# Two gated MLPs after attention: the operand sums of each layer in half steps

## The chip, the core and the metric

The kernel runs on one core of a Trainium2 chip. The engines that count here are TensorE (PE in the profile; PEld are its weight loads), VectorE (DVE), ScalarE (ACT) and the queue of SyncE that issues the DMAs (SP). Each works through its own instructions in the order written and is held up only where it waits for another. The metric is the device time of one execution in microseconds (us), lower is better.

## The reference

```python
def rmsnorm(x, g):
    return x / np.sqrt(np.mean(x * x, axis=-1, keepdims=True) + 1e-06) * g
# q, k, v: (4, 12, 448, 64)
scores = np.matmul(rmsnorm(q, g_q), rmsnorm(k, g_k).transpose(0, 1, 3, 2)) / np.sqrt(64)
attn = softmax(scores)                       # over the last axis
x = np.matmul(attn, v)                       # to (1792, 768): tokens x features
x = ((x @ w_a) * (x @ w_b)) @ w_out          # first MLP, d_ff = 1536
x = (sigmoid(x @ w_gate) * (x @ w_val)) @ w_out2   # second MLP, the same sizes
```

q, k and v are float32. The weights are float64, and the chip turns their words into float32 (the decode).

## The kernel before

**Products.** Attention runs first, then the two MLPs, each in two parts: a first part (up to the gated product) and a second part (with w_out). A matrix product is done by a seven-product scheme on 2 x 2 blocks. The first part's left operands are, with the four blocks A11, A12, A21, A22 of the transposed activations (384 features x 896 tokens each, that is KC = 3 chunks of 128 x 896): A11, A12 and A22 themselves, and S1 = A21 + A22, S2 = S1 - A11, S3 = A11 - A21, S4 = A12 - S2. To keep float32 accuracy, every operand is split in two float32r tiles, a high part (a cast on ScalarE) and a low part (operand minus high part, on VectorE): `xh`, `xl` for the left operands, `wh`, `wl` for the weights.

**Order of the products.** A list `events`, written by hand, gives the order of the products (m, p) of a first part: m is a pair of weight columns, p one of seven products. It begins (0,1), (1,1), (0,2), (2,1), (1,2), (3,1), (2,2), (3,2), (0,5), (0,6), (1,5), (0,7), (0,3), (1,6), ... Products p = 1 need A11, p = 2 A12, p = 5 S1, p = 6 S2, p = 7 S3, p = 3 S4, p = 4 A22. So the first eight work on blocks that are there, and S1 is first wanted by (0,5), S2 by (0,6). A product is six groups of three matmuls (high x high, low x high, high x low): the three chunks on 512 columns, then on 384.

**Banks.** Product (m,2) adds to the PSUM bank that (m,1) filled; between them ScalarE copies the bank into a tile `u` (line 1045, "the eviction of (m,1)"), with which line 967 later seeds the bank of (m,6). So (m,2) can't begin before the eviction of (m,1) is done. Line 1017 multiplies an odd m's result with the even one's (a gate), 1047, 1049, 1052 are other evictions.

**Weights.** `prepare` is called after each group of matmuls and writes the next step of the weights' decode (lines 693 on ScalarE, 694, 696, 700 on VectorE), of the differences of weight blocks (801, 805), and of the splits: the cast to `wh` (813, ScalarE) and `wl` (627, `rest`, VectorE).

**The operands.** `operands(l)` is a generator that writes S1 to S4 of MLP l (and, in the first MLP, a copy of A22), one chunk at a time, between the groups of matmuls: `first_part` counts the groups in `ticks` and advances the generator at every 4th, later at every 5th or 6th. Before, one advance (a step) writes: the low part of a chunk whose cast was written a step earlier, the cast of the chunk that was summed a step earlier, and this chunk's sum. `casts` and `rests` hold what is still owed. In the trace the sums are line 905, the casts line 896, the low parts line 627 (`xl`). `stage_in` loads the blocks from DRAM into the places of tiles that come to be free (`fl`, `fh` in the first MLP; `al`, `ah` are sums that the second one finds on the chip). Where the operands aren't ready when a product is written, the generator is run at once (`urgent`).

Of the kernel before, what the change touches and what calls it, by code (L numbers as in the profile page):

```python
# [14 lines left out]
ALU = mybir.AluOpType  # L15
# [8 lines left out]
def attention_then_two_gated_mlps(  # L24
# [69 lines left out]
    def place(n, half, c, dtype=F32R, name="x"):  # L94

        return places[n].tile([P, S2], dtype, tag=f"{half}{c}", name=f"{name}{half}")
# [515 lines left out]
    def take_u():  # L612
        tag = free_u.pop(0)
        return tag, ups[0].tile([P, S2], F32, tag=tag, name=tag)
# [11 lines left out]
    def rest(t, hi, lo, eng):  # L626
        eng.tensor_tensor(out=lo, in0=t, in1=f32(hi), op=ALU.subtract)  # L627
# [219 lines left out]
    def stage_in(l, n, c):  # L847

        at = where[l]
        t, half, spot, y = {"A21": (1, 0, "S4", "l"), "A11": (0, 0, "A22", "l"), "A22": (1, 1, "A22", "h"), "A12": (0, 1, "S4", "h")}[n]  # L850
        tile_ = place(at[spot], y, c, F32, "f")
        staged[l].setdefault(n, []).append(tile_)
        nc.sync.dma_start(out=tile_, in_=xd[l][t][KC * half + c])
# [24 lines left out]
    def operands(l):  # L878

        at = where[l]  # L880
        a, b, d = (staged[l][n] for n in ("A21", "A22", "A11"))
        casts, rests = [], []

        def flush(n=0):

            while rests and len(rests) + len(casts) > n:
                m, t, hi, lo, tag = rests.pop(0)
                rest(t, hi, lo, nc.vector)
                X.setdefault(m, []).append((hi, lo))
                if tag:  # L890
                    free_u.append(tag)
            while len(casts) > min(n, 1):
                m, c, t, tag = casts.pop(0)
                hi = place(at[m], "h", c)
                lo = place(at["A22" if (l, m) == (0, "S4") else "S4" if (l, m) == (0, "A22") else m], "l", c)
                nc.scalar.copy(out=hi, in_=t)
                rests.append((m, t, hi, lo, tag))
            if n == 0 and rests:
                flush()

        def to(m, c, t, tag=None):
            casts.append((m, c, t, tag))

        def tt(out, x, y, op):
            nc.vector.tensor_tensor(out=out, in0=x, in1=y, op=op)


        t = a if l == 0 else b
        for c in range(KC):
            flush(2)  # L910
            tt(t[c], a[c], b[c], ALU.add)
            to("S1", c, t[c])
            if l == 0:
                stage_in(0, "A12", c)
            yield
        for c in range(KC):
            flush(2)
            tt(t[c], t[c], d[c], ALU.subtract)
            to("S2", c, t[c])
            yield  # L920
        for c in range(KC):
            flush(2)
            if l == 0:
                tt(t[c], staged[l]["A12"][c], t[c], ALU.subtract)
                to("S4", c, t[c])
                yield
                continue
            while len(free_u) < (1 if urgent else 3):
                flush()
                yield  # L930
            tag, u = take_u()
            tt(u, d[c], a[c], ALU.subtract)
            tt(t[c], staged[l]["A12"][c], t[c], ALU.subtract)
            to("S4", c, t[c])
            yield
            flush(1)
            to("S3", c, u, tag)
            yield
        flush()
        if l == 0:  # L940
            for c in range(KC):
                while len(free_u) < 1:
                    flush()
                    yield
                flush(1)
                tag, u = take_u()
                nc.scalar.copy(out=u, in_=b[c])
                to("A22", c, u, tag)
                yield
            flush()  # L950

    ready, urgent = [False], []

    def first_part(l, then):
# [15 lines left out]
        for e, (m, p) in enumerate(events):  # L970
# [18 lines left out]
            for o, size in HALVES:  # L989
                for c in range(KC):  # L990
                    hi, lo = X[n_][c]
                    for z, (w, x) in enumerate(((wh, hi), (wh, lo), (wl, hi))):
                        nc.tensor.matmul(  # L993
                            ps[:, o:o + size], w[:, P * c:P * c + P], x[:, o:o + size],
                            start=(p in (1, 5) and c == 0 and z == 0), stop=(c == KC - 1 and z == 2),
                            skip_group_check=p not in (1, 5),
                        )
                    prepare(l, min(e + AHEAD, NE - 1), 1)
                    if more is None and ready[0]:
                        more = operands(l)  # L1000
                    if more is not None:
                        ticks += 1
                        if ticks % ((5 if ticks > 24 else 4) if l else 6 if ticks > 12 else 4) == 0:
                            next(more, None)
                    if e >= NE - 4:
                        then(e - NE)
                    yield
# [407 lines left out]
```

## Time and profile before

| | |
|---|---|
| runs shown | 1212.5, 1213.63, 1213.7 us; median 1213.63 us |
| the profiled execution | 1212.98 us; span from first to last instruction 1211.2 us |
| PE busy | 1195.3 us, 99% of the span |
| DVE busy | 918.6 us, 76% |
| ACT busy | 655.4 us, 54% |
| first MLP, first part | starts at 269.18 us |
| second MLP, first part | starts at 740.37 us |

The profiled execution's own time lies 1.78 us over its span, and 0.65 us under the median of the runs. The engines' busy times overlap. Matmuls are pipelined, so that each lasts longer in the records than the distance to the next one's start; a row's idle time in brackets is counted from the end of the one before.

### The profile page before, as it was taken

How to read it: one execution, taken by the hardware profiler on the slowest of the kernel's cores; microseconds unless marked ns; L12 is line 12 of the kernel's file. 1: busy time of each engine (PE TensorE's matmuls, PEld its weight loads, DVE VectorE, ACT ScalarE, POOL GpSimd, SP SyncE). 2: the span in 40 equal slices, each digit the busy share in tenths (PEclk: the TensorE clock that was granted, in tenths of full speed). 3: DMA queues.
4: the chain of work that ended last, by engine and by line, in shares of the span. 5: the costliest groups of instructions: out<-in, count | busy, mean ns of one | idle time of the engine just before them, and what ended most of it. 6: DMA issues, size and time to landing. Idle time of an engine off the chain costs nothing.

```text
span 1211.2 us, 18283 instructions
## 1 busy us (share of the span) xinstructions
PE 1195.3 (99%) x6468; PEld 1013.9 (84%) x6468; DVE 918.6 (76%) x1625; ACT 655.4 (54%) x1276; POOL 157.7 (13%) x241
## 2 busy tenths in 40 slices
PE   8999999999999999999999999999999999999997
PEld 6666666658788888888888888888888888999997
DVE  8888888977868687785768688976786877666672
ACT  7787788864634433444455566544545444445542
POOL 5665668600000000000000000000000000000000
PEclk9999999999999999999999999999999999999999
DMA  5444455348136465654955753234564654777683
GB/s 134 134 137 118 124 151 159 100 148 308 48 126 189 146 194 161 189 190 139 319 183 185 244 178 116 78 133 130 173 202 142 200 162 143 270 252 242 198 257 96
DMA packets 142764, 205.78 MB, mean 170 GB/s; under 512 B 23208, under 2 KB 116560, under 8 KB 142672
## 3 DMA queue, kind: packets, MB, share of 16 engines
q1 hardware_dynamic: 142064, 204.18, 53.9%
q8 instruction: 51, 0.84, 0.3%
q10 hardware_dynamic: 480, 0.43, 0.1%
q14 instruction: 41, 0.34, 0.1%
q0 software_dynamic: 128, 0.00, 0.0%
HBM read 150.21 MB, written 54.35 MB: 169 GB/s over the span
## 4 chain that ended last, share of the span: by engine, by line
PE 89%; DVE 4%; DMA 3%; ACT 2%; issue 1%; SPq 1%; ACTq 0%; DVEq 0%
PE mm L993 46%; PE mm L1276 13%; PE mm L1286 10%; PE pv L410 6%; PE s L350 5%; PE tr L381 4%; PE tr L303 1%; DVE xl L627 1%; PE tr L378 1%; DMA fh<-xd 1%; PE tr L386 1%; DMA xd<-xs 1%; DMA u<-gd 1%; DVE wl L627 0%; DMA raw<-in_moe_w_a_dram 0%
## 5 line engine op out<-in xcount | busy, mean ns | idle before, releaser
L993 PE MATMUL mm<-xl,wh 128*128 128x512 f32 (+1 forms) x1008 | 369.0, 366 | 2.6 <-DVE xl L627 2.6
L993 PE MATMUL mm<-xh,wl 128*128 128x512 f32 (+1 forms) x1008 | 370.3, 367 | 0.7 <-DVE wl L627 0.7
L993 PE MATMUL mm<-xh,wh 128*128 128x512 f32 (+1 forms) x1008 | 368.2, 365 | 0.7 <-ACT u L1045 0.5
L993 PEld LDWEIGHTS mm<-xl,wh 128*128 128x128 f32 x1008 | 189.6, 188 | 26.3 <-DVE xl L627 3.5
L993 PEld LDWEIGHTS mm<-xh,wh 128*128 128x128 f32 x1008 | 189.9, 188 | 25.0 <-issue 1.4
L993 PEld LDWEIGHTS mm<-xh,wl 128*128 128x128 f32 x1008 | 189.5, 188 | 22.1 <-DVE wl L627 1.1
L627 DVE TENSOR_TENSOR wl<-d,wh 128x384 fp32r<-128x384 f32 x250 | 136.3, 552 | 64.7 <-ACT wh L1153 40.9
L813 ACT CAST wh<-d 128x384 fp32r<-128x384 f32 x166 | 82.0, 514 | 102.0 <-DVE d L801 81.6
L693 ACT ACTIVATE d<-raw 128x384 f32<-128x384 f32 x138 | 75.7, 555 | 80.9 <-DMA raw<-in_moe_w_out_dram 40.5
L700 DVE SCALAR_TENSOR_TENSOR d<-d,raw 128x384 uint32<-128x384 uint32 x138 | 77.5, 562 | 54.7 <-ACT d L693 49.1
L368 ACT ACTIVATE P<-s,nm 128x448 f32<-128x448 f32 x168 | 105.2, 635 | 5.7 <-DVE nm L356 5.1
L1153 ACT CAST wh<-d 128x384 fp32r<-128x384 f32 x84 | 43.2, 514 | 119.6 <-issue 36.8
L356 DVE TENSOR_REDUCE nm<-s 128x1 f32<-128x448 f32 x168 | 97.3, 613 | 3.1 <-PE s L350 3.1
L1286 PE MATMUL mm<-wh,gh 128*128 128x384 f32 x294 | 98.8, 336 | 0.3 <-ACT mm L1257 0.2
L1286 PE MATMUL mm<-wl,gh 128*128 128x384 f32 x294 | 98.6, 335 | 0.0
L1286 PE MATMUL mm<-wh,gl 128*128 128x384 f32 x294 | 98.5, 335 | 0.0
L1276 PE MATMUL mm<-gl,wh 128*128 128x512 f32 x252 | 92.6, 368 | 0.0
L1276 PE MATMUL mm<-gh,wl 128*128 128x512 f32 x252 | 92.4, 366 | 0.0
L1276 PE MATMUL mm<-gh,wh 128*128 128x512 f32 x252 | 91.7, 364 | 0.0
L696 DVE SCALAR_TENSOR_TENSOR raw<-raw 128x384 uint32<-128x384 uint32 x140 | 78.1, 558 | 4.0
L397 ACT COPY pt<-tr 128x512 f32<-128x512 f32 x96 | 54.9, 572 | 44.7 <-PE tr L381 42.1
L1063 DVE TENSOR_TENSOR u<-mm,u 128x896 f32<-128x896 f32 x48 | 52.2, 1087 | 27.9 <-PE mm L993 27.9
(161 smaller groups left out, 1949.4 us busy)
## 6 DMA issues: line engine op xcount, KB each, us to landing
gd<-u SPq DMA_DIRECT2D x60, 448.0 KB
u<-gd SPq DMA_DIRECT2D x60, 448.0 KB
d<-wd SPq DMA_DIRECT2D x132, 192.0 KB
raw<-in_moe_w_out_dram SPq DMA_DIRECT2D x48, 384.0 KB
wd<-d SPq DMA_DIRECT2D x72, 192.0 KB
raw<-in_moe_w_a_dram SPq DMA_DIRECT2D x24, 384.0 KB
raw<-in_moe_w_b_dram SPq DMA_DIRECT2D x24, 384.0 KB
raw<-in_moe_w_val_dram SPq DMA_DIRECT2D x23, 384.0 KB
```

The lines of the kernel that those rows point to most:

```text
L350: nc.tensor.matmul(out_, w[e, o:o + P], x[e, m:m + S], start=(n == 0), stop=(n == 2))
L356: nc.vector.tensor_reduce(out=d["nm"][:, t:t + 1], in_=d["ps"][t], axis=AX.X, op=ALU.max, negate=True)
L368: nc.scalar.activation(out=e, in_=d["ps"].pop(t), func=AF.Exp, bias=d["nm"][:, t:t + 1], accum_out=d["sum"][:, t:t + 1])
L410: nc.tensor.matmul(d["pv"][64 * h:64 * h + 64], w, x, start=(j == 0), stop=(j == R), skip_group_check=True)
L627: eng.tensor_tensor(out=lo, in0=t, in1=f32(hi), op=ALU.subtract)
L693: nc.scalar.activation(out=f32(t), in_=f32(high), func=AF.Copy, scale=2.0 ** -112)
L696: nc.vector.scalar_tensor_tensor(out=low, in0=high, scalar=0x80000000, in1=low, op0=ALU.bitwise_and, op1=ALU.bitwise_or)
L700: nc.vector.scalar_tensor_tensor(out=t, in0=t, scalar=3, in1=low, op0=ALU.logical_shift_left, op1=ALU.bitwise_or)
L813: nc.scalar.copy(out=hi, in_=t)
L993: nc.tensor.matmul(ps[:, o:o + size], w[:, P * c:P * c + P], x[:, o:o + size], start=(p in (1, 5) and c == 0 and z == 0), stop=(c == KC - ...
L1276: nc.tensor.matmul(ps[:, o:o + size], w[:, P * un:P * un + P], g[:, o:o + size], start=(p in (1, 5) and f == 0 and z == 0), stop=(f == HF ...
L1286: nc.tensor.matmul(ps[:, o:o + HB], g[:, P * t:P * t + P], w, start=(p in (1, 5) and f == 0 and z == 0), stop=(f == HF - 1 and z == 2), sk ...
```

## The change

The generator's step is cut in two halves. In one half it writes the low part of the chunk before and the sum of this one, in the other the cast of this one. A chunk's low part then comes in the half step after its cast, and its cast in the half step after its sum: one chunk is in work at a time, where before three were. The half steps come at every 2nd group, later at every 3rd (first MLP) or at two groups of five (second MLP), so that a chunk gets as many groups as before. In the second MLP S3's difference is a half step alone, and its cast and low part come after S4's of the same chunk. The loads, the products, their order and the number of sums and casts stay as they are.

```diff
--- before.py
+++ after.py
@@ -879,75 +879,71 @@
 
         at = where[l]
         a, b, d = (staged[l][n] for n in ("A21", "A22", "A11"))
-        casts, rests = [], []
-
-        def flush(n=0):
-
-            while rests and len(rests) + len(casts) > n:
-                m, t, hi, lo, tag = rests.pop(0)
-                rest(t, hi, lo, nc.vector)
-                X.setdefault(m, []).append((hi, lo))
-                if tag:
-                    free_u.append(tag)
-            while len(casts) > min(n, 1):
-                m, c, t, tag = casts.pop(0)
-                hi = place(at[m], "h", c)
-                lo = place(at["A22" if (l, m) == (0, "S4") else "S4" if (l, m) == (0, "A22") else m], "l", c)
-                nc.scalar.copy(out=hi, in_=t)
-                rests.append((m, t, hi, lo, tag))
-            if n == 0 and rests:
-                flush()
-
-        def to(m, c, t, tag=None):
-            casts.append((m, c, t, tag))
-
-        def tt(out, x, y, op):
+        t = a if l == 0 else b
+        spare_u = lambda: len(free_u) >= (1 if l == 0 or urgent else 3)
+
+        def tt(out, x, y, op=ALU.subtract):
             nc.vector.tensor_tensor(out=out, in0=x, in1=y, op=op)
 
-
-        t = a if l == 0 else b
-        for c in range(KC):
-            flush(2)
+        def s1(c):
             tt(t[c], a[c], b[c], ALU.add)
-            to("S1", c, t[c])
             if l == 0:
                 stage_in(0, "A12", c)
+            return t[c], None
+
+        def s2(c):
+            tt(t[c], t[c], d[c])
+            return t[c], None
+
+        def s4(c):
+            tt(t[c], staged[l]["A12"][c], t[c])
+            return t[c], None
+
+        def s3(c):
+            thirds[c] = tag, u = take_u()
+            tt(u, d[c], a[c])
+            return None, None
+
+        def s3_end(c):
+            return thirds.pop(c)[::-1]
+
+        def a22(c):
+            tag, u = take_u()
+            nc.scalar.copy(out=u, in_=b[c])
+            return u, tag
+
+        jobs = [(n, f, c) for n, f in (("S1", s1), ("S2", s2)) for c in range(KC)]
+        if l == 0:
+            jobs += [(n, f, c) for n, f in (("S4", s4), ("A22", a22)) for c in range(KC)]
+        else:
+            thirds.clear()
+            jobs += [(n, f, c) for c in range(KC) for n, f in ((None, s3), ("S4", s4), ("S3", s3_end))]
+        low_at = {"S4": "A22", "A22": "S4"} if l == 0 else {}
+        last = None
+
+        def low():
+            n, u, hi, lo, tag = last
+            rest(u, hi, lo, nc.vector)
+            X.setdefault(n, []).append((hi, lo))
+            if tag:
+                free_u.append(tag)
+
+        for n, make, c in jobs:
+            if last:
+                low()
+                last = None
+            while make in (s3, a22) and not spare_u():
+                yield
+            u, tag = make(c)
+            if make is not s3_end:
+                yield
+            if u is None:
+                continue
+            hi, lo = place(at[n], "h", c), place(at[low_at.get(n, n)], "l", c)
+            nc.scalar.copy(out=hi, in_=u)
+            last = n, u, hi, lo, tag
             yield
-        for c in range(KC):
-            flush(2)
-            tt(t[c], t[c], d[c], ALU.subtract)
-            to("S2", c, t[c])
-            yield
-        for c in range(KC):
-            flush(2)
-            if l == 0:
-                tt(t[c], staged[l]["A12"][c], t[c], ALU.subtract)
-                to("S4", c, t[c])
-                yield
-                continue
-            while len(free_u) < (1 if urgent else 3):
-                flush()
-                yield
-            tag, u = take_u()
-            tt(u, d[c], a[c], ALU.subtract)
-            tt(t[c], staged[l]["A12"][c], t[c], ALU.subtract)
-            to("S4", c, t[c])
-            yield
-            flush(1)
-            to("S3", c, u, tag)
-            yield
-        flush()
-        if l == 0:
-            for c in range(KC):
-                while len(free_u) < 1:
-                    flush()
-                    yield
-                flush(1)
-                tag, u = take_u()
-                nc.scalar.copy(out=u, in_=b[c])
-                to("A22", c, u, tag)
-                yield
-            flush()
+        low()
 
     ready, urgent = [False], []
 
@@ -1000,7 +996,7 @@
                         more = operands(l)
                     if more is not None:
                         ticks += 1
-                        if ticks % ((5 if ticks > 24 else 4) if l else 6 if ticks > 12 else 4) == 0:
+                        if ticks % 5 in (0, 2) if l and ticks > 24 else ticks % (2 if l or ticks <= 12 else 3) == 0:
                             next(more, None)
                     if e >= NE - 4:
                         then(e - NE)
```

The order of the matmuls, of GpSimd's work and of the DMAs is the same in both programs. What moves stands on ScalarE and VectorE. In the rows below the number behind a tile's name tells tiles apart; numbers of lines behind `operands` are four lower after the change (1045 is 1041 there, 1017 is 1013).

ScalarE in the first MLP, around the evictions of (2,1) and (3,1); `fl_4511`, `fl_4515`, `fl_4517` are chunks 0, 1, 2 of S1 and then of S2, and `u3`, `u2` take the evictions. Before:

```order
L1052 ACTIVATE u0_4596<-mm_4421 128x896
L813 CAST wh_4602<-u4_4377 128x384
L896 CAST xh_4612<-fl_4511 128x896
L1045 COPY u3_4627<-mm_4598 128x896
L813 CAST wh_4632<-d8_4545 128x384
L896 CAST xh_4643<-fl_4515 128x896
L813 CAST wh_4666<-d0_1025 128x384
L896 CAST xh_4674<-fl_4517 128x896
L1045 COPY u2_4687<-mm_4658 128x896
```

and now:

```order
L943 CAST xh_4578<-fl_4511 128x896
L943 CAST xh_4597<-fl_4515 128x896
L1048 ACTIVATE u0_4603<-mm_4421 128x896
L813 CAST wh_4609<-u4_4377 128x384
L943 CAST xh_4623<-fl_4517 128x896
L1041 COPY u3_4637<-mm_4605 128x896
L813 CAST wh_4642<-d8_4545 128x384
L943 CAST xh_4652<-fl_4511 128x896
L813 CAST wh_4676<-d0_1025 128x384
L943 CAST xh_4683<-fl_4515 128x896
L1041 COPY u2_4697<-mm_4668 128x896
```

The eviction of (2,1) (to `u3`) came behind the cast of S1's chunk 0 and now comes behind that of S1's chunk 2; that of (3,1) (to `u2`) came behind the cast of S1's chunk 2 and now comes behind that of S2's chunk 1.

VectorE in the same stretch, from the sum of S1's chunk 2 on; `mm_4531` is the bank of (1,2), whose gate goes to `u0`, `d0_1025` is the difference of weights for (0,5), and `wl` from `u4_4377` is that of (2,2). Before:

```order
L905 TENSOR_TENSOR fl_4517<-fl_4517,fh_4519 128x896
L627 TENSOR_TENSOR wl_4603<-u4_4377,wh_4602 128x384
L627 TENSOR_TENSOR xl_4613<-fl_4511,xh_4612 128x896
L905 TENSOR_TENSOR fl_4511<-fl_4511,fl_4521 128x896
L1017 TENSOR_TENSOR u0_4596<-mm_4531,u0_4596 128x896
L801 TENSOR_TENSOR d0_1025<-d1_2377,d0_1025 128x384
```

and now:

```order
L886 TENSOR_TENSOR fl_4517<-fl_4517,fh_4519 128x896
L627 TENSOR_TENSOR xl_4624<-fl_4517,xh_4623 128x896
L886 TENSOR_TENSOR fl_4511<-fl_4511,fl_4521 128x896
L627 TENSOR_TENSOR wl_4610<-u4_4377,wh_4609 128x384
L627 TENSOR_TENSOR xl_4653<-fl_4511,xh_4652 128x896
L886 TENSOR_TENSOR fl_4515<-fl_4515,fl_4523 128x896
L1013 TENSOR_TENSOR u0_4603<-mm_4531,u0_4603 128x896
L801 TENSOR_TENSOR d0_1025<-d1_2377,d0_1025 128x384
```

Three low parts (S1's chunks 1 and 2, S2's chunk 0) and the sum of S2's chunk 1 now stand ahead of the gate and of the difference of weights behind it, which did not before; ahead of the `wl` of (2,2) it is the three low parts of S1 and the sum of S2's chunk 0.

ScalarE in the second MLP, around the eviction of (3,1) (to `u1`); `al_7806`, `al_7814`, `al_7822` are the chunks of S1, S2 and then S4, `u3`, `u5` hold S3's, `d0_8527` is the difference of weights for (0,5). Before:

```order
L896 CAST xh_8802<-al_7814 128x896
L693 ACTIVATE d3_8811<-raw_8648 128x384
L896 CAST xh_8831<-al_7822 128x896
L813 CAST wh_8844<-d0_8527 128x384
L693 ACTIVATE d5_8851<-raw_8778 128x384
L896 CAST xh_8865<-al_7806 128x896
L1045 COPY u1_8874<-mm_8836 128x896
```

and now:

```order
L943 CAST xh_8797<-al_7822 128x896
L1041 COPY u6_8800<-mm_8761 128x896
L813 CAST wh_8805<-d7_8695 128x384
L693 ACTIVATE d3_8815<-raw_8648 128x384
L943 CAST xh_8835<-al_7806 128x896
L813 CAST wh_8848<-d0_8527 128x384
L943 CAST xh_8853<-u3_8810 128x896
L693 ACTIVATE d5_8859<-raw_8786 128x384
L1041 COPY u1_8878<-mm_8840 128x896
```

The casts ahead of the eviction were those of S2's chunks 1 and 2 and S4's chunk 0, with the weights' casts and decodes between; they now are those of S2's chunk 2, S4's chunk 0 and S3's chunk 0.

## Rows read from the trace of the kernel before

**Rows 1.** Page: busy time by engine; chain that ended last, shares of the span.

```profile
PE 1195.3 (99%) x6468; PEld 1013.9 (84%) x6468; DVE 918.6 (76%) x1625; ACT 655.4 (54%) x1276; POOL 157.7 (13%) x241
...
PE 89%; DVE 4%; DMA 3%; ACT 2%; issue 1%; SPq 1%; ACTq 0%; DVEq 0%
```

**Rows 2.** TensorE in order of time, first MLP: start us, us, line, operation [idle before <-releaser].

```profile
295.60 0.39 PE L993 MATMUL mm<-xh,wh 128*128 128x512 f32 x1
...
299.27 0.48 PE L993 MATMUL mm<-xh,wh 128*128 128x512 f32 x1
...
306.68 0.39 PE L993 MATMUL mm<-xh,wh 128*128 128x512 f32 x1
...
309.24 0.50 PE L993 MATMUL mm<-xl,wh 128*128 128x512 f32 x1 [1.47 <-DVE xl L627]
...
311.36 0.68 PE L993 MATMUL mm<-xl,wh 128*128 128x512 f32 x1 [1.16 <-DVE xl L627]
...
315.06 0.39 PE L993 MATMUL mm<-xh,wh 128*128 128x512 f32 x1
```

**Rows 3.** Stretches of 5 us: busy time (xinstructions) by engine, granted clock, DMA share, GB/s.

```profile
305.00:310.00 5.00, 3.53 (x18) 2.68 (x16) 4.96 (x7) 3.08 (x5) 0.00 (x0) 1.00 0.38 132
310.00:315.00 5.00, 3.84 (x12) 3.45 (x12) 4.96 (x7) 3.38 (x5) 0.00 (x0) 0.66 0.01 4
...
775.00:780.00 5.00, 4.31 (x21) 3.50 (x20) 4.96 (x9) 3.13 (x6) 0.00 (x0) 1.00 0.37 131
```

**Rows 4.** TensorE in order of time, second MLP.

```profile
762.31 0.40 PE L993 MATMUL mm<-xh,wh 128*128 128x512 f32 x1
...
766.60 0.50 PE L993 MATMUL mm<-xh,wh 128*128 128x512 f32 x1 [0.46 <-ACT u L1045]
...
782.86 0.39 PE L993 MATMUL mm<-xh,wh 128*128 128x512 f32 x1
```

**Rows 5.** VectorE in order of time, first MLP.

```profile
286.33 1.09 DVE L905 TENSOR_TENSOR fl<-fl,fh 128x896 f32<-128x896 f32 x1 [1.91 <-DMA fl<-xd]
...
289.50 1.09 DVE L905 TENSOR_TENSOR fl<-fl,fh 128x896 f32<-128x896 f32 x1 [2.08 <-DMA fl<-xd]
...
295.37 1.08 DVE L1017 TENSOR_TENSOR u<-mm,u 128x896 f32<-128x896 f32 x1
296.38 0.55 DVE L801 TENSOR_TENSOR d<-d,d 128x384 f32<-128x384 f32 x1
296.84 0.55 DVE L627 TENSOR_TENSOR wl<-d,wh 128x384 fp32r<-128x384 f32 x1
```

**Rows 6.** ScalarE in order of time, first MLP.

```profile
287.45 0.95 ACT L896 CAST xh<-fl 128x896 fp32r<-128x896 f32 x1 [1.27 <-DVE fl L905]
...
297.03 0.51 ACT L813 CAST wh<-d 128x384 fp32r<-128x384 f32 x1 [5.46 <-DVE d L801]
297.45 0.94 ACT L896 CAST xh<-fl 128x896 fp32r<-128x896 f32 x1
298.29 0.90 ACT L1045 COPY u<-mm 128x896 f32<-128x896 f32 x1
```

**Rows 7.** VectorE in order of time, second MLP.

```profile
740.72 0.55 DVE L696 SCALAR_TENSOR_TENSOR u<-u 128x384 uint32<-128x384 uint32 x1
...
762.30 1.08 DVE L1017 TENSOR_TENSOR u<-mm,u 128x896 f32<-128x896 f32 x1
763.30 0.55 DVE L801 TENSOR_TENSOR d<-d,d 128x384 f32<-128x384 f32 x1
```

**Rows 8.** ScalarE in order of time, second MLP.

```profile
750.08 1.28 ACT L1052 ACT_TABLE_LOAD   x1
...
763.94 0.52 ACT L813 CAST wh<-d 128x384 fp32r<-128x384 f32 x1 [5.30 <-DVE d L801]
764.36 0.56 ACT L693 ACTIVATE d<-raw 128x384 f32<-128x384 f32 x1
...
765.65 0.90 ACT L1045 COPY u<-mm 128x896 f32<-128x896 f32 x1
```

## Prediction

> **What bounds the kernel now.** I read the page first. TensorE is busy for 99% of the span, and yet the chain that ended last names it for 89% only; the rest is mostly VectorE, DMA and ScalarE [rows 1]. The reader is to see that there are few places in which TensorE is not the bound. Following the chain in order of time, they lie where an MLP begins, while its operand sums are made. So I read TensorE there, product by product. In the first MLP product (2,2) begins at 295.60 and (3,2) at 299.27: a product takes 3.67 us when nothing holds it. Product (0,6) begins at 306.68 and the next, (1,5), at 315.06 only, after 8.38 us. It waits twice for the low parts of S2, for 1.47 and 1.16 us [rows 2]. Of the 4.7 us that are lost some 3.0 are these waits (the stretches without a start are a little longer than the idle in brackets), and 1.75 are slow matmuls behind them: in the 5 us from 310 the granted clock is 0.66 in the mean, between the levels of 2.4 and 1.2 GHz [rows 3]. In the second MLP (2,2) begins at 762.31 and (0,7) at 782.86. These are five products, 18.3 us if unhindered, and took 20.55, so 2.25 us are lost; the first of these waits, 0.46 us at the start of (3,2), is for a copy from PSUM by ScalarE, the eviction of (3,1) [rows 4]. There the clock stays at 1.00 [rows 3]. All else in the kernel is TensorE at its pace, so the change can win at most some 7 us, and what it makes TensorE lose in the two stretches is added in full.
>
> **The change: what it removes and what it costs.** No sum, cast or low part is added or removed, and no load. Only the order on VectorE and ScalarE changes. A sum or low part of 896 columns takes VectorE 1.09 us, with 1.0 us from start to start; one of 384 columns 0.55 and 0.46 [rows 5]. A cast takes ScalarE 0.94 (start to start 0.84), an eviction 0.90, a cast of weights 0.51 (0.42), a decode step 0.56 (0.46) [rows 6, 8]. From a sum's end to its cast's start it is 0.03 us (287.42 to 287.45) [rows 5, 6]; I take the same for the way back. So sum, cast, low part, next sum need 1.09 + 0.03 + 0.94 + 0.03 + 1.0 = 3.1 us when they follow each other directly, and VectorE has only 2 us of work of its own in it. Before, the three stood a step apart and VectorE did other sums meanwhile.
>
> **First MLP.** The sums of S1's chunks 0 and 1 start at 286.33 and 289.50, when their loads land [rows 5]; the change leaves the loads alone. From there I go by the order. Chunk 1's sum ends at 290.6, its cast at 291.6, its low part runs from there to 292.7. Chunk 2: sum 292.6 to 293.7, cast to 294.7, low part from 294.7. S2's chunk 0: sum at 295.7, cast 296.8 to 297.8, in between the `wl` of (2,2), 296.7 to 297.25, then the low part at 297.8. S2's chunk 1: sum at 298.8. Only then come the gate of (1,2) at 299.8, which now starts at 295.37, and the difference of weights at 300.8 to 301.35, now 296.38 [rows 5]. ScalarE waits for that difference, as it does now for 5.46 us [rows 6]; behind it stand the cast of S2's chunk 1 (301.9) and the eviction of (3,1), which so runs from 302.7 to 303.6 where it now starts at 298.29 [rows 6].
>
> TensorE loses twice. Product (2,2) needs its `wl` with its third matmul, 0.46 us after 295.60; it gets it at 297.3: 1.25 us. Product (3,2) adds to the bank that the eviction reads, so it starts at 303.7 and not at 299.27: 4.4 us lost in all [rows 2]. The low parts of S2 then come at 303.9 to 307, before (0,6) asks for them at about 311, and the wait that stands there now is gone. The seed of (0,6) is copied by 310.8, the `wl` of (1,5) is ready at 314.5 and wanted at 315.1: both in time. The clock is the open price. After two waits with some work between it fell and cost 1.75 us, after waits of under a microsecond it did not fall [rows 2, 3, 4]. The gap before (3,2) is one of 3.1 us, closer to the former, and I take 1.75; the other end is nothing. So 4.4 + 1.75 - 4.7 = 1.4 us more than now, or 0.3 less without the clock.
>
> **Second MLP.** The sum of S1's chunk 0 now stands right behind the decode step at 740.72 [rows 7]: 741.2 to 742.3, cast to 743.25, low part; chunk 1: sum at 744.3, three short steps of the weights, low part at 747.0; chunk 2: sum 748.0, cast to 750.05, low part 750.1; S2's chunk 0: sum 751.1, cast to 753.15. Then ScalarE loads its table (1.28 us [rows 8]), does the sigmoid and two short steps, and the cast of S2's chunk 1 is late, 756.1 to 757.05, though its sum is done at 755.25. Its low part follows at 757.15, the sum of chunk 2 at 758.15, cast to 760.2, low part at 760.25, S3's difference at 761.25, two decode steps, S4's sum at 763.1, a decode step, the gate of (1,2) at 764.6, the difference of weights at 765.6 to 766.15. Now these two are at 762.30 and 763.30 [rows 7]. ScalarE: the weights' cast at 766.25, the cast of S3's chunk 0, a decode step, the eviction of (3,1) from 767.95 to 768.85; now it starts at 765.65 [rows 8]. Product (3,2) so begins at 768.9 instead of 766.60 [rows 4]. In the same way the seed of (0,6) is done at 777.45, where TensorE would be there at 776.3, and the `wl` of (1,5) at 782.25, wanted at 781.6. Product (0,7) begins at 785.5 instead of 782.86 [rows 4]: 2.6 us more. If the clock falls after the gap before (3,2), that costs nothing more, since (0,6) and (1,5) wait for VectorE and ScalarE anyway, for as long.
>
> **Sum.** 1.4 + 2.6 = 4.0 us, on the profiled execution's 1212.98 us 1217.0. That execution lies 0.65 us under the median of the runs, so I say 1217.2. Each of the two stretches may be off by 0.5 us, since some thirty hand-overs are summed.
>
> All of this rests on ScalarE not letting an eviction past a cast that still waits. The rows show it: a cast that could run stands behind the one that waits 5.46 us and starts right after it [rows 6]. The Trainium skill says the same, in PSUM — Partial Sum Buffer, section Engine vs sequencer instructions: the queues of ScalarE, VectorE and GpSimd are strictly first in, first out. By that rule the sum is the one above. Were evictions let past, (3,2) would start in time in both MLPs, the first would lose 1.25 us and not 4.7, the second at most what it loses now, and the kernel would take some 1209.5 us.
>
> **The rivals.** (a) The same waits, but the clock holds in the first MLP: 4.4 - 4.7 + 2.6 = 2.3 us more, 1215.5 us, on the edge of what can be told. For it: the clock held in the second MLP. Against it: the gap is longer than all that are there now. (b) It is faster. The mechanism would be that S2's low parts come before (0,6) and that VectorE catches up in its idle times, so that both evictions are in time. The whole 4.7 us and perhaps 1 us of the second MLP would be won: 1207 to 1209 us. It decides itself at the eviction of (3,1): it must end by 299.2 in the first MLP. For it: VectorE idles 1.91 and 2.08 us before the first two sums [rows 5], and one low part now falls into the second of these pauses. Against it: from 305 to 315 VectorE has no pause to catch up in (4.96 of each 5 us busy [rows 3]), and the waits for casts are new. The Trainium skill, in Perfetto Trace Analysis, section Optimizing Scalar/DVE Operations, says that breaking up instructions may let work end sooner where ScalarE and VectorE hold others up without being saturated; its condition fails here by the 4.96 of 5 us. (c) Worse: the clock falls in both MLPs and the chain comes out a microsecond longer in each, 1220 us.
>
> **How the numbers follow.** A difference of 0.2%, 2.4 us, is about what a measurement of this kernel can tell from no change. Forecast (clock falls once): 0.52. Rival (a): 0.28. Rival (b): 0.09. Rival (c): 0.07. The rest, 0.04, that the times come out within 1 us of now by errors that cancel. Slower by over 0.2%: 0.52 x 0.95 of the forecast, 0.07, and 0.45 of (a), that is 0.69. Faster: 0.08 of (b). Same: the remaining 0.23. The range leaves out (b), most of the upper end of (c), and takes in (a) with its error downward: 1213.4 to 1219.6.
>
> **What would show it.** Right: a row of TensorE at the start of (3,2) in each MLP with some 3 us of idle, put down to ScalarE's eviction (line 1041), and none for `xl` at (0,6); the gate of (1,2) at about 299.8 and 764.6; a granted clock below 1 at about 304 to 307. Wrong: an eviction of (3,1) that ends before 299.3, or a low part of S1's chunk 2 well before 294.7, which would mean that the chain above has a step too many.

## The result, and the profile after

The changed kernel takes 1219.23 us (median of 6 runs, 1218.4 to 1221.84), the kernel before 1213.07 us in runs made beside it (6 runs, 1211.52 to 1214.05). The ratio is 1.0053, with a 95% interval of 1.0042 to 1.0065: slower by 6.2 us. Forecast were 1217.2 us and a range from 1213.4 to 1219.6: the measured time lies 2.0 us over the forecast and 0.4 us under the upper end of the range. The profiled execution is the slowest of the six: 1221.84 us, span 1220.1 us.

The page after: busy time by engine, and the chain that ended last. TensorE's share of the chain has gone from 89% to 87%, its busy time is nearly the same [rows 1].

```profile
PE 1196.3 (98%) x6468; PEld 1014.0 (83%) x6468; DVE 918.9 (75%) x1625; ACT 655.7 (54%) x1276; POOL 157.0 (13%) x241
PE 87%; DVE 5%; ACT 3%; DMA 2%; issue 1%; SPq 1%; ACTq 0%; DVEq 0%
```

TensorE of the changed kernel in order of time, first MLP, only rows with idle time in front. Lines behind the generator are 4 lower than before: 989 are the products, 1041 the eviction of (m,1), 1045 that of (0,6).

```profile
289.12 0.50 PE L989 MATMUL mm<-xh,wl 128*128 128x512 f32 x1 [0.50 <-DVE wl L627]
296.74 0.50 PE L989 MATMUL mm<-xh,wh 128*128 128x512 f32 x1 [0.49 <-ACT u L1041]
298.53 0.67 PE L989 MATMUL mm<-xh,wl 128*128 128x512 f32 x1 [1.07 <-DVE wl L627]
304.89 0.50 PE L989 MATMUL mm<-xh,wh 128*128 128x512 f32 x1 [1.32 <-ACT u L1041]
321.12 0.50 PE L989 MATMUL mm<-xh,wh 128*128 128x512 f32 x1 [1.30 <-ACT u L1045]
```

The rows at 296.74, 304.89 and 321.12 are the starts of (2,2), (3,2) and (0,7). Nothing waits for `xl` at (0,6) any more, which before cost 1.47 and 1.16 us [rows 2]; but (3,2) begins at 304.89 instead of 299.27, and (0,7) waits for the eviction of (0,6), which it did not before. From (0,6) to (1,5) it is now 3.67 us, a product that nothing holds, where it was 8.38:

```profile
312.32 0.39 PE L989 MATMUL mm<-xh,wh 128*128 128x512 f32 x1
...
315.99 0.39 PE L989 MATMUL mm<-xh,wh 128*128 128x512 f32 x1
```

The first sum of S1 begins when its load has landed (VectorE):

```profile
287.50 1.09 DVE L886 TENSOR_TENSOR fl<-fl,fh 128x896 f32<-128x896 f32 x1 [3.76 <-DMA fl<-xd]
```

How VectorE and ScalarE get there is read best from the chain of waits between 295 and 306 us (start, length, what):

```profile
294.94 0.95 ACT xh L943
295.89 0.02 issue
295.92 1.09 DVE xl L627
297.01 1.01 DVE fl L886
298.02 0.02 issue
298.04 0.95 ACT xh L943
298.99 0.02 issue
299.01 1.09 DVE xl L627
300.11 1.00 DVE fl L886
301.11 0.06 DVE u L1013
...
302.03 0.56 DVE d L801
```

Cast, low part, sum, cast, low part, sum: they follow one another with 0.02 us between them, about 3.1 us a round. Behind the second round stand the gate (1013) and the difference of weights (801), and ScalarE, which waits for the difference, reaches the eviction of (3,1) only after one more cast. ScalarE there:

```profile
302.69 0.51 ACT L813 CAST wh<-d 128x384 fp32r<-128x384 f32 x1 [3.70 <-DVE d L801]
303.10 0.93 ACT L943 CAST xh<-fl 128x896 fp32r<-128x896 f32 x1
303.94 0.90 ACT L1041 COPY u<-mm 128x896 f32<-128x896 f32 x1
```

Before, the last of these began at 298.29 [rows 6]. The eviction of (0,6), for which (0,7) waits, is the last of these rows of ScalarE; ahead of it stand a cast of S4 that waits for its sum, and a copy of A22:

```profile
318.48 0.94 ACT L943 CAST xh<-fl 128x896 fp32r<-128x896 f32 x1 [0.95 <-DVE fl L886]
319.32 0.94 ACT L912 COPY u<-fh 128x896 f32<-128x896 f32 x1
320.17 0.90 ACT L1045 COPY u<-mm 128x896 f32<-128x896 f32 x1
```

In the second MLP TensorE waits at the starts of (3,2) and (0,6) and once for `wl`:

```profile
771.59 0.50 PE L989 MATMUL mm<-xh,wh 128*128 128x512 f32 x1 [2.97 <-ACT u L1041]
780.22 0.50 PE L989 MATMUL mm<-xh,wh 128*128 128x512 f32 x1 [1.03 <-ACT mm L963]
785.00 0.50 PE L989 MATMUL mm<-xh,wl 128*128 128x512 f32 x1 [0.42 <-DVE wl L627]
```

The matmuls come in the same order in both kernels, so the two traces can be laid side by side and the distance of each matmul to its counterpart read off. The changed kernel enters the first MLP 0.28 us earlier (268.65 against 268.93) and is 2.40 us later at (0,7) (321.12 against 318.72): 2.68 us lost. Its distance is 2.49 us at the second MLP's (3,1) and 5.44 at (0,7) (788.30 against 782.86): 2.95 us lost. At 1123.55 us, near the end, TensorE waits 1.92 us for `al` (line 1297) and then runs at a lower clock, together 3.4 us; nothing that the change touches is there. The copy to `al` begins at 1122.70. VectorE waits 1.61 us for a load of gated products before its sum at 1118.20, and from there sums, a low part and a cast on ScalarE lead to that copy; the profile's chain names a load of weights (`d<-wd`) that landed at 1122.67. Which of the two loads held it is not shown.

### The profile page after: what moved, and what is told of

It reads as the page before. It is cut to its first block, busy times and chain, and to the rows that moved or that the text cites. A ratio compares the mean times of both kernels' runs of the same rounds, so it can differ in the third digit from the quotient of the medians.

```text
span 1220.1 us, 18276 instructions
## 1 busy us (share of the span) xinstructions
PE 1196.3 (98%) x6468; PEld 1014.0 (83%) x6468; DVE 918.9 (75%) x1625; ACT 655.7 (54%) x1276; POOL 157.0 (13%) x241
## 4 chain that ended last, share of the span: by engine, by line
PE 87%; DVE 5%; ACT 3%; DMA 2%; issue 1%; SPq 1%; ACTq 0%; DVEq 0%
PE mm L989 44%; PE mm L1272 13%; PE mm L1282 10%; PE pv L410 6%; PE s L350 6%; PE tr L381 4%; PE tr L303 1%; DVE xl L627 1%; PE tr L378 1%; DMA wd<-d 1%; ACT xh L943 1%; DVE fl L886 1%; DMA fl<-xd 1%; DVE al L886 1%; PE tr L386 1%
```

## The experiments

**The theory:** TensorE is held up where ScalarE must evict (3,1) (and in the first MLP (0,6)), because half steps make VectorE wait for each cast and put casts ahead of evictions. **Rivals:** the late load and the clock made the difference; or the two MLPs act on each other; or half steps are as such too many. Below, "lost in the first MLP" is the growth of the distance to before from the first whole product to (0,7), "in the second" that from (3,1) to (0,7), both read from the profiles as above, one execution each, so that they scatter more than the medians do; "behind it" is the growth from there to the last matmul. Times are medians; ratios are against the kernel before in runs on the same chip, estimated from all the runs, and not quotients of the medians.

| kernel | us | ratio (95%) | first MLP | second MLP | behind it |
|---|---|---|---|---|---|
| changed | 1219.23 | 1.0053 (1.0042 to 1.0065) | +2.68 | +2.95 | +3.4 |
| half steps in the first MLP | 1216.39 | 1.0021 (1.0013 to 1.0030) | +1.92 | 0.00 | 0.1 |
| half steps in the second MLP | 1217.31 | 1.0035 (1.0023 to 1.0047) | -0.99 | +4.09 | -0.4 |
| half steps held back | 1219.81 | 1.0045 (1.0033 to 1.0057) | +1.18 | +2.93 | 0.2 |
| sum ahead of the low part | 1213.31 | 0.9996 (0.9987 to 1.0005) | -1.74 | -0.05 | -0.1 |
| both of these | 1210.31 | 0.9972 (0.9961 to 0.9984) | -2.73 | -0.05 | -0.4 |
| S3 joined with S4 | 1223.50 | 1.0085 (1.0072 to 1.0099) | +3.14 | +7.01 | 0.1 |
| before, S2 first | 1208.83 | 0.9961 (0.9949 to 0.9973) | -4.79 | -0.02 | 0.7 |
| the same, S3 on GpSimd | 1211.15 | 0.9979 (0.9970 to 0.9988) | -4.56 | +1.73 | 0.3 |
| before, S2 first in both | 1208.13 | 0.9953 (0.9941 to 0.9966) | -4.71 | -1.35 | 1.0 |

**Half steps in one MLP alone.** Both generators are in the kernel (lines behind them are 70 higher than before); the rhythm is that of the generator.

```diff
-                        more = operands(l)
+                        more = (operands if l == 0 else operands_whole)(l)
```

> The half steps in the first MLP alone; the second MLP keeps the whole steps of before. Theory (each MLP loses by itself, where an eviction stands behind the casts and differences that half steps put ahead of it): product (0,7) of the first MLP begins 2.4 to 2.7 us later than before, from then on the distance to before stays, and the time is 1213.1 + 2.5 = 1215.6 us. Rival 1 (part of the first MLP's loss was a load of the first sum that landed 1.2 us later in the one profiled execution): (3,2) begins at about 303.7 instead of 304.9, +1.2 us, 1214.3. Rival 2 (the two MLPs are not independent, the wait of 1.92 us in the last part comes from the first MLP's change): 1218 or more.

> The half steps in the second MLP alone; the first keeps the whole steps of before. Theory: (0,6) of the first MLP waits for xl as before; in the second (3,2) waits about 3 us for the eviction and (0,7) is 2.9 us later than before, 1213.1 + 2.9 = 1216.0 us. Rival (the wait of 1.92 us and the 1.5 us behind it in the last part of the profiled changed kernel belong to the half steps of the second MLP): 1213.1 + 2.9 + 3.5 = 1219.5 us, with a load of gated products landing after 1118 us in the profile.

With half steps in the first MLP alone, that MLP loses 1.92 us in the profile and nothing changes afterwards; with half steps in the second alone, it loses 4.09. So each loses by itself, and rival 2 of the first falls. Rival 1 was half right: S1's first load landed at 286.79 instead of 287.50, by 0.71 us earlier, and (3,2) began at 304.18 instead of 304.89, by the same 0.71. Its 1214.3 us did not come: the median is 1216.39, and the profiled execution (1214.79 us) the fastest of eleven. The sum and the start of (3,2):

```profile
286.79 1.09 DVE L960 TENSOR_TENSOR fl<-fl,fh 128x896 f32<-128x896 f32 x1 [2.34 <-DMA fl<-xd]
304.18 0.50 PE L1063 MATMUL mm<-xh,wh 128*128 128x512 f32 x1 [2.89 <-ACT u L1115]
```

The clock was at 1.00 there throughout, and yet (3,2) was just as late: the chain sets its start, not the clock. In the second kernel the wait near 1120 us is missing, so the half steps of the second MLP do not bring it by themselves. The 4.09 us there are 1.1 more than in the changed kernel: 0.3 of them are there when (3,2) begins, after a wait of 3.31 us, and 0.8 come behind it, where the clock had fallen to 0.50 (mean of 770 to 775). These two kernels' differences from before, by the ratios 2.5 and 4.3 us, add up to 6.8 us, against 6.2 for both together, within the intervals.

**Half steps held back.** In the first MLP S2's chunk 1 is summed and cast behind the gate of (1,2) and the eviction of (3,1) in the written order.

```diff
-  if ticks % 5 in (0, 2) if l and ticks > 24 else ticks % (2 if l or ticks <= 12 else 3) == 0:
+  if ticks % 5 in (0, 2) if l and ticks > 24 else (not l and ticks in (25, 28, 29, 31)) or (l or ticks not in (21, 24, 27, 30)) and ticks % (2 if l or ticks <= 12 else 3) == 0:
```

> The changed kernel, with three half steps of the first MLP moved a few groups later: the low part of S2's chunk 0 with the sum of chunk 1, and its cast, come behind the gate of (1,2), the weight difference and the eviction of (3,1) on their engines; the next two half steps follow closer. Theory (the eviction of (3,1) was late because these stood ahead of it): the gate begins at about 298.5 instead of 301.0, the eviction at 300.4 instead of 303.9, product (3,2) no longer waits for it and begins at 302 (303 if the clock falls) instead of 304.9: 2 to 3 us less than the changed kernel, 1216 to 1217 us. Rival (the late load of the first sum and the clock set the start of (3,2)): within 0.7 us of the changed kernel, 1218.5 to 1219.5 us. Second rival (what is won there is given back at (0,6), whose low parts come later): the same time, but with waits for xl at (0,6).

The gate began at 298.15 and the eviction at 300.22 as expected, and (3,2) at 301.60 without a wait. But later the seed of (0,6) (line 963) and the eviction of (0,6) (1045) came late. ScalarE and TensorE:

```profile
300.22 0.90 ACT L1041 COPY u<-mm 128x896 f32<-128x896 f32 x1
...
309.42 0.93 ACT L943 CAST xh<-fl 128x896 fp32r<-128x896 f32 x1
310.26 0.90 ACT L963 COPY mm<-u 128x896 f32<-128x896 f32 x1
```

```profile
311.21 0.50 PE L989 MATMUL mm<-xh,wh 128*128 128x512 f32 x1 [2.12 <-ACT mm L963]
320.49 0.50 PE L989 MATMUL mm<-xh,wh 128*128 128x512 f32 x1 [1.69 <-ACT u L1045]
```

Of the 4.2 us by which (3,2) begins earlier (each counted from the start of the MLP), 1.5 were left at (0,7) in the profile, and the time is not measurably lower (1.0045 and 1.0053, intervals that overlap). The cause at (3,2) is shown; the second rival holds for the time, with the seed in the place of `xl`. It looks as if VectorE were late as a whole, and moving work out of the way of one wait only handed the delay to the next.

**The sum ahead of the low part.** If VectorE is late as a whole because it waits for casts, it should be given something to do in that time: the next chunk's sum.

```diff
-            if last:
+            if last and make in (s3, s3_end, a22):
                 low()
                 last = None
             while make in (s3, a22) and not spare_u():
                 yield
             u, tag = make(c)
+            if last:
+                low()
+                last = None
```

> The changed kernel with one thing turned round in its first kind of half step: the next chunk's sum is written ahead of the low part of the chunk before (not at S3's difference and the copies of A22, which need a free buffer), so that VectorE does the sum while ScalarE casts. Theory (VectorE loses about 0.5 to 1.1 us per chunk in waiting for a cast, 2.75 us in four waits up to the eviction of (3,1), and everything behind is late by this): the waits for xh on VectorE are gone, the eviction of (3,1) in the first MLP starts near 301.5 instead of 303.9, (3,2) near 302.5, and with the same in the second MLP 3 to 4 us less than the changed kernel: 1215 to 1216 us. Rival (as in the kernel with held back half steps, what is won at (3,2) is given back at (0,6) and (0,7)): within 1 us of the changed kernel, 1218.5 to 1220 us.

Sum and low part turned round take back the whole loss: 1213.31 us, not to be told from before, and 1.7 us under the 1215 us that were expected at best. VectorE's waits for `xh` between 286 and 325 us fall from 6.8 us in nine to 2.3 us in two. The waits of the changed kernel, then of this one (engine, line, released by: us in all, times, longest):

```profile
DVE xl L627 <- ACT xh L943: 6.8, 9, 1.1
```

```profile
DVE xl L627 <- ACT xh L946: 2.3, 2, 1.3
```

The eviction of (3,1) starts at 301.14, near the 301.5 expected. It is still late, behind a cast of S2 (300.30), and (3,2) waits 2.27 us for it. That the time equals that of before is a coincidence: one loss at (3,2), 2.95 us, stands in the place of another at (0,6), 4.7 us. The profiled execution, the fastest of eleven (1210.97 us), is 1.74 us ahead at (0,7); where the slower ones lose this is not shown. The rival falls: (0,6) and (0,7) of the first MLP wait for nothing.

**Both edits at once**, the sum ahead and the half steps held back.

> The changed kernel with both edits at once: the sum ahead of the low part in a half step, and the three half steps of the first MLP held back until the eviction of (3,1) is written. Theory (half steps cost nothing by themselves; what costs is VectorE's wait for casts and a cast ahead of the eviction): in the first MLP the eviction starts before 299.5 us, no wait at (3,2) and (0,6), and 2 to 3 us less than with the sum ahead alone (1213.3 us): 1210.3 to 1211.3 us. Rival (as with the held back half steps alone, the seed of (0,6) and the eviction before (0,7) take over): 1212.5 to 1214 us.

The eviction starts at 299.24 and holds (3,2) no more, and 1210.31 us is 3 us under the sum ahead alone and faster than before (0.9972). Half steps as such need not cost time, then. The seed of (0,6) is again late, by 0.91 us, so the rival was right about the place and wrong about the size. The Trainium skill (Perfetto Trace Analysis, section Optimizing Scalar/DVE Operations) says that breaking up instructions may let work be completed sooner where ScalarE and VectorE aren't saturated but cause bubbles on other engines. No run here shows this, since the instructions kept their sizes and only the step that writes them was split. Of that split the order decided: as it was made it gave 1.0053, with sum and low part turned round and three half steps held back 0.9972.

**S3's difference joined with S4's sum** in one half step, in the second MLP, as before.

```diff
-            if make is not s3_end:
+            if make not in (s3, s3_end):
                 yield
```

> The changed kernel, but in the second MLP S3's difference is written in one half step with S4's sum, as before, instead of in one of its own. Theory (where the difference stands changes nothing that TensorE waits for, the wait is made by the casts and low parts of S1 and S2): (3,2) and (0,7) of the second MLP begin as late as in the changed kernel within 0.7 us, 1218.5 to 1220 us. Rival (the half step of its own pushed the gate and the evictions back): 2 us less, about 1217 us.

Neither came true: it is 4 us slower than the changed kernel. One yield less, and every later half step is written earlier; now a cast of S4's chunk 1, which waits 2.46 us for its sum, stands in front of the eviction of (3,1), and (3,2) waits 6.71 us. ScalarE and TensorE:

```profile
774.56 0.94 ACT L943 CAST xh<-al 128x896 fp32r<-128x896 f32 x1 [2.46 <-DVE al L886]
775.41 0.90 ACT L1041 COPY u<-mm 128x896 f32<-128x896 f32 x1
```

```profile
776.36 0.80 PE L989 MATMUL mm<-xh,wh 128*128 128x512 f32 x1 [6.71 <-ACT u L1041]
```

In the changed kernel the eviction is at 770.65 and that cast at 775.94. So S3's half step of its own is the part of the change that helped: it keeps one more cast behind the eviction.

**Before, S2 first.** The whole steps of before; only S2's casts and low parts are finished ahead of S4's sums in the first MLP, and the copies of A22 wait for two free buffers.

```diff
             to("S2", c, t[c])
             yield
+        if l == 0:
+            flush()
+            yield
...
-                while len(free_u) < 1:
+                while len(free_u) < (1 if urgent else 2):
```

> The kernel before with one thing moved: in the first MLP the low parts and last casts of S2 are all written in a step of their own ahead of S4's sums (and the copies of A22 wait until two buffers are free). Theory (before, the 4.7 us at (0,6) were lost because S4's sums stood ahead of S2's low parts on VectorE, not because VectorE lacked time): no wait for xl at (0,6), the clock stays at 1.00, 1213.1 - 4.7 = 1208.4 us. Rival 1 (VectorE is full there, the gate and the weight differences behind the three low parts come 1 to 2 us late and hold TensorE instead): 1211 to 1213 us. Rival 2 (S4 is now late at (0,3)): 1213 us or more.

All 4.7 us of the first MLP are won: 1208.83 us. VectorE writes S2's three low parts without a break, then the gate:

```profile
304.03 3.19 DVE L627 TENSOR_TENSOR xl<-fl,xh 128x896 fp32r<-128x896 f32 x3
307.14 1.08 DVE L1020 TENSOR_TENSOR u<-mm,u 128x896 f32<-128x896 f32 x1
```

Before, two sums of S4, which is wanted three products after S2, and a gate (with the weights' work behind it) stood between them, and TensorE waited for the second and third [rows 2]:

```profile
303.57 1.08 DVE L627 TENSOR_TENSOR xl<-fl,xh 128x896 fp32r<-128x896 f32 x1
304.68 1.09 DVE L905 TENSOR_TENSOR fl<-fh,fl 128x896 f32<-128x896 f32 x1
305.69 1.08 DVE L1017 TENSOR_TENSOR u<-mm,u 128x896 f32<-128x896 f32 x1
...
308.10 1.08 DVE L627 TENSOR_TENSOR xl<-fl,xh 128x896 fp32r<-128x896 f32 x1
309.21 1.09 DVE L905 TENSOR_TENSOR fl<-fh,fl 128x896 f32<-128x896 f32 x1
310.22 1.08 DVE L627 TENSOR_TENSOR xl<-fl,xh 128x896 fp32r<-128x896 f32 x1
```

VectorE was as full as ever (4.98 of the 5 us from 305, before 4.96), but with the right work. The late gate held nothing: no product of the first MLP waits.

**The same with S3's differences on GpSimd**, in the second MLP, `nc.gpsimd.tensor_tensor` for `nc.vector.tensor_tensor`.

> The kernel before with S2's low parts ahead of S4's sums in the first MLP, and in the second MLP S3's three differences on GpSimd, which has nothing to do there. Theory (the 2.25 us that the second MLP loses come from a full VectorE, 97% busy; three instructions of 1.09 us less there let the evictions, the seed and the low part of the weights come in time): some 1.5 to 2.2 us less than the version without, 1206.6 to 1207.3 us. Rival 1 (a difference takes GpSimd 2.15 us by the nearest row, S3 is late at (0,7) or VectorE is slowed meanwhile): 1208.8 us or more. Rival 2 (the waits there come from ScalarE's order, not from VectorE's load): 1208.8 us, unchanged.

Rival 1, by its second half: 2.3 us slower than without, and (3,2) of the second MLP waits 2.10 us where it waited 0.46. VectorE is held while GpSimd works. GpSimd, then VectorE (start, length):

```profile
735.48 4.53 POOL L935 TENSOR_TENSOR u<-al,ah 128x896 f32<-128x896 f32 x2 [488.68 <-ACT ah L1316]
764.07 2.71 POOL L935 TENSOR_TENSOR u<-al,ah 128x896 f32<-128x896 f32 x1 [24.06 <-DMA gd<-u]
```

```profile
735.82 2.21 DVE L700 SCALAR_TENSOR_TENSOR d<-d,raw 128x384 uint32<-128x384 uint32 x1 [1.66 <-ACT d L693]
737.96 2.28 DVE L694 TENSOR_SCALAR u<-u 128x384 uint32<-128x384 uint32 x1
...
764.72 3.01 DVE L905 TENSOR_TENSOR al<-ah,al 128x896 f32<-128x896 f32 x1
```

These three take 0.56, 0.35 and 1.09 us when GpSimd is idle. The second ends 0.2 us after the two differences on GpSimd, the third 1.0 us after the later one. The Trainium skill (SBUF — State Buffer, section "SBUF: two separate sides") says that the two engines share a pair of ports which an instruction locks for its whole length; the rows agree.

**Before, S2 first in both MLPs**: the condition `if l == 0` taken out.

> The kernel before with S2's low parts and last casts written ahead of S4's sums (in the second MLP: ahead of S3's differences and S4's sums) in both MLPs; the copies of A22 wait for two free buffers. Theory (the second MLP loses its 2.25 us by the same cause: sums that are wanted late stand on VectorE ahead of the gate and the weight difference that ScalarE waits for before it evicts (3,1)): gate and difference of the second MLP come about 2 us earlier, no wait at (3,2), and the time is 1 to 2 us under the 1208.8 us of the version with the first MLP alone: 1207 to 1208 us. Rival (the work only moves later, and the seed of (0,6), the low part of the weights at (1,5) or S3 at (0,7) is late instead): 1208.5 to 1211 us.

1208.13 us: 0.7 us under the version with the first MLP alone, between theory and rival, and not apart from that version by the intervals. The theory's way was wrong: the gate of the second MLP comes not 2 us earlier but 1.0 later (759.15 against 758.15, with the MLP begun at the same time), and (3,2) still waits. VectorE, then TensorE:

```profile
759.15 1.08 DVE L1019 TENSOR_TENSOR u<-mm,u 128x896 f32<-128x896 f32 x1
```

```profile
762.61 0.50 PE L995 MATMUL mm<-xh,wh 128*128 128x512 f32 x1 [0.62 <-ACT u L1047]
```

What is won in the profile, 1.35 us up to (0,7) of the second MLP, is won behind (3,2), where (0,6) and (1,5) no longer wait (0.29 and 0.69 us without this edit); 0.65 are given back within (0,7), where S3's low part is late (0.38 us of waiting): the rival in part. It is the fastest kernel of the study, 0.47% under before.

## Why the prediction was right, point by point

The mechanism and the side were right, and of the sum of 4.0 us measured were 5.4 on the path of the profile (2.68 + 2.95, less the 0.28 of an earlier start) and 6.2 by the medians. The terms were not all sized as they came out, and added to the median of 1213.63 us that it names, the 4.0 us give 1217.6 and not 1217.2.

- **The round of 3.1 us** (sum, cast, low part, next sum) was right and is the cause: with sum and low part turned round the loss is gone.
- **The eviction of (3,1), first MLP**: forecast 302.7, it came at 303.94. The chain was right step by step; its start was not. The first load landed at 287.50 and not at 286.33. In the profiles of the other kernels that sum began between 286.00 and 288.53, so this is a scatter of the load, and the chain passes it on in full: in the three kernels whose first MLP is written alike (changed, half steps in the first MLP, S3 joined) it began at 287.50, 286.79 and 288.53, and (3,2) 17.39 us later each time. Forecast were 17.37 (286.33 to 303.7).
- **The gain at (0,6)**, 4.7 us forecast, came: the distance to before falls from 5.65 us at (0,6) (312.32) to 0.93 at (1,5) (315.99).
- **The clock, 1.75 us**: the mis-sized term. The clock did fall, to 0.50 from about 299 to 302, in (2,2) and not in (3,2), after waits of 0.49 and 1.07 us, and cost nothing: the slow matmuls ended before the eviction that TensorE had to wait for in any case. (Of the three kernels with the same first MLP the clock fell there in two, and the 17.39 us are the same in all.) That is why (3,2) shows 1.32 us of idle and not the 3 us that the prediction wanted to see; with the clock at 1.00 the row said 2.89.
- **The step that was missed**: product (0,7) adds to the bank that (0,6) filled, and the eviction of (0,6) (line 1045, at 320.17) stands behind S4's late cast and a copy of A22. It cost 1.5 us, with the 0.1 us of restart. The prediction followed the seed and the `wl` beyond (3,2), but not this eviction. (Nor did it follow that of (2,1), for which (2,2) waited 0.49 us; the wait at (3,2) hides this.) With the late load it fills the gap that the clock term left: 1.4 - 1.75 + 1.2 + 1.5 = 2.35, against 2.68 measured, of which 0.28 are the earlier start. That the total came near is thus partly luck: errors of both signs cancelled.
- **Second MLP**: 2.6 us forecast, 2.95 measured. Less the 2.49 us by which the kernel entered, the gate was at 764.8 (forecast 764.6), the eviction at 768.2 (767.95), (3,2) at 769.1 (768.9), the seed at 776.8 (its end at 777.7, forecast 777.45), (0,7) at 785.8 (785.5). That a fall of the clock there costs nothing was too strong: with half steps in the second MLP alone it cost 0.8 us, in the kernel with held back steps, where it was shorter, nothing.
- **First in, first out on ScalarE** held in every run: evictions were late by what stood ahead of them, and moved when it was moved.
- **Rival (b)**: its 4.7 us in the first MLP were there to be kept, by other means: not by smaller steps but by writing S2's low parts ahead of S4's sums.

What stays open is the rest between 5.4 and 6.2 us. The wait near 1123 us, 3.4 us in the profiled execution, comes behind late loads and differs from kernel to kernel: it cost 0.7 us at the same place in the kernel with S2 first, whose second MLP is that of before, and 0.2 us or nothing in the six other kernels with half steps. Whether the changed kernel meets it more often was not measured.

## What to carry to other kernels

Where one engine's work goes through another and comes back (sum, cast, low part), write the next independent item between the two halves; here the waits for the round trip fell from 6.8 to 2.3 us, and turning sum and low part round was worth 6 us. Before work is cut finer, ask in which order it is wanted: the 4.7 us of the first MLP were lost to sums and a gate that were wanted later than the low parts behind them. And where an eviction frees a bank that TensorE adds to next, list what stands ahead of it in its engine's order, for every product that has one.

## What the runs showed of the hardware

The clock of TensorE doesn't fall after each wait of one length. In the kernel before, and in the one with half steps in the second MLP alone, whose first MLP is written as before, (0,6) waits for the same two low parts, 1.47 and 1.16 us. In the first the granted clock then fell to 0.50 (2.4 to 1.2 GHz) and 0.66 was the mean of 310 to 315; in the second, which had waited 0.38 us at (3,2) besides, it stayed at 1.00. TensorE of the second kernel there, and its clock (the third number from the end):

```profile
310.25 0.50 PE L1063 MATMUL mm<-xl,wh 128*128 128x512 f32 x1 [1.47 <-DVE xl L627]
312.38 0.50 PE L1063 MATMUL mm<-xl,wh 128*128 128x512 f32 x1 [1.16 <-DVE xl L627]
```

```profile
310.00:315.00 5.00, 3.58 (x17) 2.93 (x18) 4.93 (x7) 4.13 (x6) 0.00 (x0) 1.00 0.12 40
```

In the three kernels whose half steps of the first MLP are alike the waits in (2,2) are 0.49 and 1.07, 0.49 and 1.06, and 0.47 and 1.07 us; the clock fell to 0.50 behind them in the first and the third and stayed at 1.00 in the second. So waits that are alike cost 1.75 us of clock in one execution and nothing in another; what decides is not shown. And the fall costs nothing where the next wait would have held TensorE as long anyway.
